# A gated convolution and token-mixing kernel: a new fixed order of the same operations, and some row work moved between VectorE and ScalarE

## The chip, the cores and the metric

The kernel runs on one core of a Trainium2 chip. A core has five engines that work side by side: TensorE (PE, matrix products), VectorE (DVE), ScalarE (ACT), GpSimd (POOL) and SyncE (SP), which here only issues transfers. Sixteen DMA engines move data between memory and the core's buffer; SP's transfers go through the queue called q1 in the profile, POOL's through q0. The metric is the device time of one execution in microseconds (us), the median of several runs.

## The reference

All inputs are bf16. S is 2048, D is 640, F is 1536. With x = q:

```python
# A: shift convolution of k, times v, then a long convolution per channel
k_shift = sum over t<4 of  k_pad[:, t:t+S] * shift_k[:, 3-t]
kv      = k_shift * v
y       = irfft(rfft(kv, 2S) * rfft(ssm_k, 2S))[:S]  +  kv * ssm_D
a       = q * y
# B: an MLP over the tokens
h = (x - mean) / sqrt(var + 1e-5)              # layernorm of each row
u = gelu(einsum("bsd,sf->bdf", h, w1) + b1)    # 2048 -> 1536
b = transpose(einsum("bdf,fs->bds", u, w2) + b2)
g = sigmoid(sum(x * gate_w))
out = g * a + (1 - g) * b
```

## The kernel before, in words

**How the work is tiled.** Rows of the 2048 tokens are spread over 128 partitions in four groups hk = 0 to 3 of four rows each, so that one tile of X holds 4 × 640 values per partition. The convolution is done by a 4096-point transform written as matrix products with two tables, FTB (forward) and GTB (back), split in four residues p = 0 to 3. The filter ssm_k comes in channel-major order and has to be transposed first (tiles wT, on PE, then copied out of PSUM by DVE or ACT).

**Stages, in the order in which they bind.**

1. Filter: load `ssm` in two halves of 1024 (each in two loads, of 2 and 3 channel blocks), transpose it (`transp`), transform it (`fwd`, `fwd_even`) into the tiles C. Beside it DVE takes the row statistics of X (`ln_tile`, L884 and L887), POOL raises the variance to −1/2 (`ln_scale`, sd and rstd), and DVE or ACT normalise the sixteen rows in place (`ln_apply`). POOL also makes the four gate factors KF.
2. The shifted k (`k_turn`, `kv`), its product with v, and the transform of that, with its sums over residues (`mixing`, `mixing_acc`; some of these sums are made by POOL, as transfers that add into their destination).
3. MLP, first product (m1): 12 tiles of F, each in 4 steps of 8 matmuls (L1083), with w1 in two ring buffers, ring0 and ring1, loaded in blocks c = 0, 1, 2 of four loads hk each (`w1_load`). ACT applies GELU into GT.
4. MLP, second product (m2): 16 tiles of the output, each in 6 steps of 4 matmuls (L1122), with w2 in the tile W2, loaded in two halves of six loads each (L1111). DVE meanwhile multiplies the two transforms (`product`, `cross`, `invmix`) and POOL adds pieces into C by accumulating transfers of 640 KB.
5. The transform back (`inverse`), times q and the gates, added to the MLP's result, stored in seven pieces and by four accumulating transfers.

W2 lies in the memory of ring0 and ring1 (W2's first 16 blocks are ring0, its last 16 are ring1). A load of W2 can therefore be issued only when the steps that read the old contents have ended: steps of m1 for the first contents, steps of m2 for the second half of w2.

**What sets the order.** `_build` makes a list of 712 operations. `_ORDER` is one list of their numbers, and `follow` (L299 on) puts the operations into that order; `emit` hands them out one by one, each to its engine's instruction stream, so an engine executes its operations in the order in which `_ORDER` names them. `_SLOTS` gives each of the 133 PSUM tiles one of four slots. `TAKES` says, for work that either DVE or ACT can do, which takes it: wT00 to wT14 (copies of transposed tiles out of PSUM, first digit the half), ln0 to ln15 (a layernorm row), kp0 to kp3 (a turn of k). `_Tracker` finds every overlap of buffers and puts the semaphore waits in; a wait stands in the stream of the engine that needs it, and whatever follows in that stream stays behind it. The helper lines that appear in the profile: L298 matmul, L267 accumulating transfer from POOL, L272 transfer from SP, L603 ACT, L559 and L573/L574 DVE or POOL, L613 a DVE copy out of PSUM.

Numbers of operations that are named further on:

| numbers | what |
|---|---|
| 4, 5, 6, 7 | SP loads of X for hk 0 to 3 |
| 8, 9 and 12, 13 | SP loads of ssm, first half and second half |
| 10, 11 | SP loads of FTB |
| 226 | POOL memset of KT, the border of the turned k |
| 237 | SP load of w1, block 1, hk 0 (ring1); read first by m1 step 419 |
| 244, 245, 297, 299 | POOL accumulating transfers into C, stage 2 |
| 394 to 397 | SP loads of w1, block 2, hk 0 to 3 (ring0); 394 is read first by m1 step 435 |
| 458 to 463 | SP loads of W2, first half |
| 520 to 525 | SP loads of W2, second half |
| 602, 607, 611 to 614, 619 | POOL accumulating transfers into C, stage 4 |
| 540 to 574 | m2 steps of the output tiles 9 to 15, among them 558, 569, 570, 571, 572 |

Of the kernel before, what the change touches and what calls it, by code (L numbers as in the profile page):

```python
# [13 lines left out]
ACT = mybir.ActivationFunctionType  # L14
# [5 lines left out]
class _Tracker:  # L20
# [235 lines left out]
    def dma(self, stream, out_ap, in_ap, semname, transpose=False, noncontig=False, accum=False, wait=()):  # L256
        reads = [in_ap] + ([out_ap] if accum else [])
        writes = [out_ap]
        if wait:
            self.pre(stream, list(wait), [])  # L260
        acc = self.pre(stream, reads, writes)
        engobj = self.eng[stream]
        sem = self.dma_sems[semname]
        if transpose:
            ins = engobj.dma_start_transpose(out_ap, in_ap)
        elif accum:
            ins = engobj.dma_start(out_ap, in_ap, accum_op=ALU.add, max_dma_last_dim=2560)  # L267
        elif noncontig:
            with self.nc.allow_non_contiguous_dma(reason="tiny"):
                ins = engobj.dma_start(out_ap, in_ap)  # L270
        else:
            ins = engobj.dma_start(out_ap, in_ap)  # L272
        ins.then_inc(sem, 16)
        self.dma_cnt[semname] += 16
        v = self.dma_cnt[semname]
        self.dma_hist[(semname, v)] = dict(self.known[stream])
        src = ("dma", semname, v)
        for reg, mode in acc:
            self.add_record(reg, mode, src)
        return v  # L280
# [128 lines left out]
def bass_gated_mix__ssm_conv_h3__mixer_token_mlp__prompt_kernel(  # L409
    nc, A_q, A_k, A_v, A_shift_k, A_ssm_k, A_ssm_D, B_x, B_w1, B_b1, B_w2, B_b2, gate_w, out  # L410
):
    with nc.Block() as blk:

        @blk.tensor
        def _(pe_engine):
            _build(nc, A_q, A_k, A_v, A_shift_k, A_ssm_k, A_ssm_D, B_x, B_w1, B_b1, B_w2, B_b2, gate_w, out)
# [24 lines left out]
def _build(nc, A_q, A_k, A_v, A_shift_k, A_ssm_k, A_ssm_D, B_x, B_w1, B_b1, B_w2, B_b2, gate_w, out):  # L441
    Bsz, S, D = A_q.shape
    F = B_w1.shape[1]
# [8 lines left out]
    with ExitStack() as es:  # L452
# [13 lines left out]
        def alloc(name, shape, dtype, at=None):  # L466
            size = mybir.dt.size(dtype)
            for s_ in shape[1:]:
                size *= s_
            if at is None:  # L470
                off = cur[0]
                cur[0] = (off + size + 63) // 64 * 64
            else:
                off = at
            assert off % 4 == 0 and off + size <= top, f"SBUF overflow {name}: {off}+{size} > {top}"
            h = nc.alloc_sbuf_tensor_at(name, list(shape), dtype, offset=off)
            T.reg_sbuf(h, off)
            return h
# [36 lines left out]
        ring = [alloc(f"ring{i}", [128, 16, 512], BF16) for i in range(2)]  # L515
# [90 lines left out]
        def either(name, default):  # L606

            return TAKES.get(name, default)

# [35 lines left out]
        def dma(o, i, nbytes, stream="SP", prio=None, sem=None, rate=365.0, tok=None, **kw):  # L645
            if sem is None:
                sem = f"d{ndma[0]}"
                ndma[0] += 1
            if sem not in T.dma_sems:
                T.add_dma_sem(sem, es.enter_context(nc.semaphore(f"s_{sem}")))  # L650
            rd = [i] + ([o] if kw.get("accum") else [])
            o_ = SC.add(stream, nbytes / rate / 1000.0, lambda s: T.dma({"QA": "ACT"}.get(stream, stream), o, i, sem, **kw), rd, [o], prio=prio, lat=-1.0, name="dma")
            if tok is not None:
                toks[tok] = o_
            return o_

        def dr(t, off, ap):
            return bass.AP(tensor=t.tensor, offset=t.offset + off, ap=ap)
# [22 lines left out]
            dma(X[:, hk, :, :], row8(A_q, hk), 128 * 5120, tok=f"x{hk}", rate=400.0)  # L681

        def w1_load(c, hk):
            dma(ring[c % 2][:, 4 * hk:4 * hk + 4, :], dr(B_w1, (1024 * (hk // 2) + 4 * (hk % 2)) * F + 512 * c, [[8 * F, 128], [F, 4], [1, 512]]), 128 * 4096, tok=f"w{c}{hk}")

        def k_load(hk):
            dma(kn[hk % 2][:, :, :], row8(A_k, hk), 128 * 5120, tok=f"k{hk}")
# [24 lines left out]
            dma(o, i, nbytes, stream=stream, **kw)  # L712

        SSM0 = ((0, 2), (2, 5))
        TAKES = {'wT00': 'DVE', 'wT01': 'DVE', 'wT02': 'ACT', 'wT03': 'ACT', 'wT04': 'ACT', 'ln0': 'ACT', 'ln1': 'DVE', 'ln2': 'DVE', 'ln3': 'DVE', 'ln4': 'DVE', 'ln5': 'ACT', 'ln6': 'DVE', 'ln7': 'DVE', 'ln8': 'ACT', 'ln9': 'ACT', 'ln10': 'ACT', 'ln11': 'DVE', 'ln12': 'ACT', 'ln13': 'ACT', 'ln14': 'ACT', 'ln15': 'DVE', 'kp0': 'DVE', 'kp1': 'DVE', 'wT10': 'ACT', 'wT11': 'DVE', 'wT12': 'ACT', 'wT13': 'ACT', 'wT14': 'ACT', 'kp2': 'DVE', 'kp3': 'ACT'}
        ORDER = "x0 s00 s02 x1 f0 f1 x2 x3 s10 s12 w00 w01 k0 k1 w02 w03 gw t0 t1 v0 v1 k2 k3 v2 v3 t2 t3 w10 w11 w12 w13 g w20 w21 w22 w23".split()
        LNSEQ = "s0 s1 a0 s2 a1 s3 a2 a3".split()
        LB = [0, 4, 8, 12, 16]
# [27 lines left out]
        for a, b in SSM1:  # L746
            ssm_load(1, a, b)
        w1_load(0, 0)
        w1_load(0, 1)

        zz = alloc("zz", [128, 512], BF16, at=base_of(GTB))
# [22 lines left out]
        for hk in range(2, 4):  # L774
            w1_load(0, hk)
# [294 lines left out]
        for ft in range(FT):  # L1070
# [16 lines left out]
            if ft in (1, 3, 5, 7):  # L1087
                hk = ft // 2
# [235 lines left out]


_ORDER = """
# [24 lines left out]
"""  # L1351
_SLOTS = "0323102030032211332223111230122113203310203131102102333312112310102123021121020211023120332002313302211002332213013220303301330301031"
# [1 line left out]
_INS = ['A_q', 'A_k', 'A_v', 'A_shift_k', 'A_ssm_k', 'A_ssm_D', 'B_x', 'B_w1', 'B_b1', 'B_w2', 'B_b2', 'gate_w']  # L1354
_OUTS = [((1, 2048, 640), 'bfloat16')]
# [23 lines left out]
```

## Time and profile before

| | before |
|---|---|
| median of 3 runs | 190.12 us (189.32 to 190.36) |
| profiled execution | 190.56 us, of which the span in the profile is 188.7 us |
| mean granted clock of TensorE | 0.982 |
| PE busy | 173.8 us, 92% of the span |
| DVE busy | 167.6 us, 89% |
| ACT busy | 113.0 us, 60% |
| POOL busy | 42.4 us, 22% |
| DMA | 45.60 MB, mean 242 GB/s |

The profile is of one execution. A row of a group names line, engine, operation, the tiles written and read, the count, the busy time, the mean length of one in ns, and the idle time before it with what ended it. Instructions overlap on an engine, so busy time divided by the count says how far apart they start. The view of slices gives 40 equal parts of the span (4.7 us each) in tenths. A time to landing runs from the issue of a transfer to its last byte.

### The profile page before, as it was taken

The page shows a single profiled execution, that of the slowest core. Times are in us where ns is not written, and L with a number is a line of the kernel's source. Part 1 is how long each engine was busy: PE and PEld are TensorE (multiplying, and loading weights), DVE is VectorE, ACT ScalarE, POOL GpSimd, SP SyncE. Part 2 cuts the span into 40 slices and gives each one's busy share as a digit, 9 for nine tenths or more (in the row PEclk, how much of TensorE's full clock was granted, in tenths as well). Part 3 has the DMA queues.
Part 4 walks back from the last instruction along what each step waited for, and adds up shares of the span by engine and source line. Part 5 has one row for each costly group of instructions (what it writes and reads, how often), then busy time and mean ns, then how long its engine had stood idle before and what let it go on. Part 6 is the DMA issues. An engine that isn't in the chain of part 4 may idle for free.

```text
span 188.7 us, 3258 instructions
## 1 busy us (share of the span) xinstructions
PE 173.8 (92%) x1347; PEld 133.0 (70%) x1348; DVE 167.6 (89%) x198; ACT 113.0 (60%) x176; POOL 42.4 (22%) x42
## 2 busy tenths in 40 slices
PE   7989888999999999997999999999956799999992
PEld 2657524786677667765777778999954499987782
DVE  2799989999899997999999999999999999009894
ACT  2589999999999999977163040041500105088780
POOL 1591067000005053003311102137300000005500
PEclk9999999999999999999999999999998599999999
DMA  4999999999799999999994629999999997004998
GB/s 172 373 407 401 389 221 213 390 416 200 132 295 309 221 203 196 196 260 345 196 190 129 122 47 367 268 237 205 187 236 255 318 416 310 0 0 72 204 278 285
DMA packets 32202, 45.60 MB, mean 242 GB/s; under 512 B 11705, under 2 KB 21050, under 8 KB 32188
## 3 DMA queue, kind: packets, MB, share of 16 engines
q1 hardware_dynamic: 26384, 32.94, 53.2%
q0 software_dynamic: 5744, 12.45, 37.2%
q8 instruction: 10, 0.16, 0.3%
q14 instruction: 4, 0.03, 0.0%
q10 hardware_dynamic: 60, 0.01, 0.0%
HBM read 27.70 MB, written 2.62 MB: 161 GB/s over the span
## 4 chain that ended last, share of the span: by engine, by line
PE 58%; ACT 18%; DMA 15%; DVE 5%; POOL 2%; issue 1%; DVEq 0%; SPq 0%
PE pp L298 58%; DMA W<-in_B_w_dram 9%; ACT C L603 6%; DMA ring<-in_B_w_dram 5%; ACT ksh L603 5%; ACT X L603 3%; DVE stats L884 2%; POOL rstd L559 2%; ACT wT L603 2%; ACT kp L698 1%; DVE C L559 1%; ACT GT L603 1%; DVE wT L613 1%; DVE kp L694 0%; DVE O L619 0%
## 5 line engine op out<-in xcount | busy, mean ns | idle before, releaser
L559 DVE TENSOR_TENSOR C<-C 128x2560 bf16<-128x2560 bf16 (+2 forms) x47 | 61.2, 1344 | 1.7 <-ACT C L603 1.4
L298 PE MATMUL pp<-GT,W 128*128 128x320 bf16 x384 | 57.5, 309 | 5.4 <-DMA W<-in_B_w_dram 5.4
L298 PEld LDWEIGHTS pp<-GT,W 128*128 128x128 bf16 x384 | 52.3, 146 | 9.5 <-DMA W<-in_B_w_dram 6.6
L298 PE MATMUL pp<-X,ring 128*128 128x320 bf16 x384 | 55.2, 299 | 1.3 <-DMA ring<-in_B_w_dram 1.0
L298 PEld LDWEIGHTS pp<-X,ring 128*128 128x128 bf16 x384 | 37.1, 98 | 16.4 <-DMA ring<-in_B_w_dram 1.3
L603 ACT ACTIVATE C<-pp 128x640 bf16<-128x640 f32 x64 | 40.5, 735 | 1.3 <-PE pp L298 1.1
L603 ACT ACTIVATE O<-pp,c,omg 128x640 bf16<-128x640 f32 x15 | 12.9, 881 | 42.3 <-PE pp L298 42.1
L267 POOL DMA_DIRECT2D C<-C x10 | 12.3, 1372 | 51.9 <-DVE C L559 45.2
L603 ACT ACTIVATE GT<-pp,cc 128x640 bf16<-128x640 f32 x12 | 9.6, 798 | 18.5 <-PE pp L298 18.5
L298 PE MATMUL pp<-wT,FTB 128*128 128x320 bf16 x112 | 17.9, 301 | 2.9 <-ACT C L603 1.4
L298 PEld LDWEIGHTS pp<-wT,FTB 128*128 128x128 bf16 x112 | 9.2, 97 | 11.1 <-ACT C L603 6.1
L559 DVE TENSOR_TENSOR tm<-C,C 128x2560 bf16<-128x2560 bf16 (+1 forms) x7 | 14.3, 2055 | 0.0
L603 ACT ACTIVATE cgb<-pp,gg 128x640 bf16<-128x640 f32 x16 | 12.2, 791 | 3.1 <-PE pp L298 1.8
L267 POOL DMA_DIRECT2D O<-q_hi x4 | 4.8, 1324 | 39.3 <-DVE q_hi L559 39.2
L884 DVE BATCH_NORM_STATS2 stats<-X 128x6 f32<-128x320 bf16 x32 | 13.2, 468 | 0.0
L559 DVE TENSOR_TENSOR q_hi<-cgb,q_hi 128x1280 bf16<-128x1280 bf16 x4 | 3.2, 822 | 10.1 <-ACT cgb L603 10.1
L267 POOL DMA_DIRECT2D C<-q_hi x6 | 5.9, 977 | 26.9 <-DVE q_hi L559 16.7
L559 DVE TENSOR_TENSOR SS<-C 128x2560 bf16<-128x2560 bf16 x8 | 11.7, 1483 | 0.0
L603 ACT ACTIVATE gq<-gq 128x640 bf16<-128x640 bf16 x16 | 11.7, 745 | 0.0
L559 DVE TENSOR_TENSOR C<-tm 128x2560 bf16<-128x2560 bf16 (+1 forms) x9 | 10.5, 1191 | 0.0
L603 ACT ACTIVATE ksh<-pp 128x1024 bf16<-128x1024 f32 (+1 forms) x12 | 10.4, 883 | 0.0
L298 PE MATMUL pp<-C,GTB 128*128 128x320 bf16 x64 | 9.8, 299 | 0.0
(72 smaller groups left out, 183.9 us busy)
## 6 DMA issues: line engine op xcount, KB each, us to landing
C<-C POOLq DMA_DIRECT2D x10, 640.0 KB, 8.9
ring<-in_B_w_dram SPq DMA_DIRECT2D x12, 512.0 KB, 9.3
W<-in_B_w_dram SPq DMA_DIRECT2D x12, 512.0 KB, 8.4
X<-in_A_q_dram SPq DMA_DIRECT2D x4, 640.0 KB, 9.6
kn<-in_A_k_dram SPq DMA_DIRECT2D x4, 640.0 KB, 12.8
out_dram<-O SPq DMA_DIRECT2D x7, 320.0 KB, 3.5
C<-SS POOLq DMA_DIRECT2D x3, 640.0 KB, 9.4
ssm<-in_A_ssm_k_dram SPq DMA_DIRECT2D x2, 768.0 KB, 9.1
```

The lines of the kernel that those rows point to most:

```text
L267: ins = engobj.dma_start(out_ap, in_ap, accum_op=ALU.add, max_dma_last_dim=2560)
L298: ins = self.nc.tensor.matmul(ps_ap, lhsT=lhsT, rhs=rhs, start=start, stop=stop, skip_group_check=True)
L559: o_ = SC.add(eng, d, lambda s: T.op(eng, lambda e: e.tensor_tensor(o, a, b, op), rd, [o]), rd, [o], prio=prio, name="tt")
L603: return T.op("ACT", lambda e: e.activation(o, src, func, **kw), rr + [src], ww)
L613: return T.op("DVE", lambda e: e.tensor_copy(o, src), [src], [o])
L698: o_ = SC.add("ACT", act_dur(2560), lambda s: T.op("ACT", lambda e: e.activation(ov, iv, ACT.Copy), [i[:, :, :]], [o[:, :, :]]), [i[:, :, ...
L884: ops.append(SC.add("DVE", 0.38, (lambda o, i: lambda s: T.op("DVE", lambda e: e.bn_stats(o, i), [i], [o]))(o, i), [i], [o]))
```

## The change

The order of the operations is a new one, and with it the PSUM slots. No operation is added or taken away, and no transfer changes its size. `TAKES` moves two transposed tiles from DVE to ACT (wT00, wT01), six layernorm rows from ACT to DVE (ln0, 5, 8, 9, 10, 14) and two from DVE to ACT (ln11, ln15). `w1_load` gets a rate, an operand that only states a duration for the drawing up of an order.

```diff
         def w1_load(c, hk):
-            dma(ring[c % 2][...], dr(B_w1, ...), 128 * 4096, tok=f"w{c}{hk}")
+            dma(ring[c % 2][...], dr(B_w1, ...), 128 * 4096, tok=f"w{c}{hk}", rate=325.0)
...
-        TAKES = {'wT00': 'DVE', 'wT01': 'DVE', 'wT02': 'ACT', 'wT03': 'ACT', 'wT04': 'ACT', 'ln0': 'ACT', 'ln1': 'DVE', 'ln2': 'DVE', 'ln3': 'DVE', 'ln4': 'DVE', 'ln5': 'ACT', 'ln6': 'DVE', 'ln7': 'DVE', 'ln8': 'ACT', 'ln9': 'ACT', 'ln10': 'ACT', 'ln11': 'DVE', 'ln12': 'ACT', 'ln13': 'ACT', 'ln14': 'ACT', 'ln15': 'DVE', 'kp0': 'DVE', ...}
+        TAKES = {'wT00': 'ACT', 'wT01': 'ACT', 'wT02': 'ACT', 'wT03': 'ACT', 'wT04': 'ACT', 'ln0': 'DVE', 'ln1': 'DVE', 'ln2': 'DVE', 'ln3': 'DVE', 'ln4': 'DVE', 'ln5': 'DVE', 'ln6': 'DVE', 'ln7': 'DVE', 'ln8': 'DVE', 'ln9': 'DVE', 'ln10': 'DVE', 'ln11': 'ACT', 'ln12': 'ACT', 'ln13': 'ACT', 'ln14': 'DVE', 'ln15': 'ACT', 'kp0': 'DVE', ...}
...
 _ORDER = """
-8 0 9 4 10 5 7 11 1 13 12 20 16 6 25 21 26 226 28 2 14 32 17 22 23 3 18 24 33 39 34 30 35 42 31 19 36 86 37 40 38 43
+4 0 8 1 20 16 9 21 2 32 17 23 5 3 10 6 7 11 13 12 94 26 36 90 45 14 18 88 25 19 97 15 34 91 27 92 96 39 37 35 22 87 93
...
-_SLOTS = "0323102030032211332223111230122113203310203131102102333312112310102123021121020211023120332002313302211002332213013220303301330301031"
+_SLOTS = "0331012303123112030221232321132013112002011211120100110301033011020310301031031300202300332231122033100233121200323113121020330030323"
```

What this does to the queues that issue transfers, in words:

- SP, start: X for hk 0 goes first, then ssm's first half, X for hk 1, the first table, X for hk 2 and 3, the second table, and then ssm's second half. Before it was ssm's first half, X 0, table, X 1 and 3, table, ssm's second half, X 2.
- SP, rings: 237 is issued last of its four loads (before first), 394 last of its four.
- SP, W2: 463 goes ahead of 461 and 462. The second half is issued as 520, 522, 523, 521, 524, 525 (before 520 to 525 in turn).
- POOL: the memset of KT goes behind the first rstd; the last five accumulating transfers of stage 4 ahead of the transform back go 613, 619, 614, 612, 611 (before 613, 619, 612, 614, 611).
- PE: the steps of m1, m2 and the transforms are interleaved anew. The number of matmuls between the step that frees a part of W2 and the step that first reads its new contents changes with that.

More of the change, by code (lines that the diff above doesn't have):

```diff
@@ L683, in w1_load @@
         def w1_load(c, hk):
-            dma(ring[c % 2][:, 4 * hk:4 * hk + 4, :], dr(B_w1, (1024 * (hk // 2) + 4 * (hk % 2)) * F + 512 * c, [[8 * F, 128], [F, 4], [1, 512]]), 128 * 4096, tok=f"w{c}{hk}")
+            dma(ring[c % 2][:, 4 * hk:4 * hk + 4, :], dr(B_w1, (1024 * (hk // 2) + 4 * (hk % 2)) * F + 512 * c, [[8 * F, 128], [F, 4], [1, 512]]), 128 * 4096, tok=f"w{c}{hk}", rate=325.0)
         def k_load(hk):
@@ L714, in _build @@
         SSM0 = ((0, 2), (2, 5))
-        TAKES = {'wT00': 'DVE', 'wT01': 'DVE', 'wT02': 'ACT', 'wT03': 'ACT', 'wT04': 'ACT', 'ln0': 'ACT', 'ln1': 'DVE', 'ln2': 'DVE', 'ln3': 'DVE', 'ln4': 'DVE', 'ln5': 'ACT', 'ln6': 'DVE', 'ln7': 'DVE', 'ln8': 'ACT', 'ln9': 'ACT', 'ln10': 'ACT', 'ln11': 'DVE', 'ln12': 'ACT', 'ln13': 'ACT', 'ln14': 'ACT', 'ln15': 'DVE', 'kp0': 'DVE', 'kp1': 'DVE', 'wT10': 'ACT', 'wT11': 'DVE', 'wT12': 'ACT', 'wT13': 'ACT', 'wT14': 'ACT', 'kp2': 'DVE', 'kp3': 'ACT'}
+        TAKES = {'wT00': 'ACT', 'wT01': 'ACT', 'wT02': 'ACT', 'wT03': 'ACT', 'wT04': 'ACT', 'ln0': 'DVE', 'ln1': 'DVE', 'ln2': 'DVE', 'ln3': 'DVE', 'ln4': 'DVE', 'ln5': 'DVE', 'ln6': 'DVE', 'ln7': 'DVE', 'ln8': 'DVE', 'ln9': 'DVE', 'ln10': 'DVE', 'ln11': 'ACT', 'ln12': 'ACT', 'ln13': 'ACT', 'ln14': 'DVE', 'ln15': 'ACT', 'kp0': 'DVE', 'kp1': 'DVE', 'wT10': 'ACT', 'wT11': 'DVE', 'wT12': 'ACT', 'wT13': 'ACT', 'wT14': 'ACT', 'kp2': 'DVE', 'kp3': 'ACT'}
         ORDER = "x0 s00 s02 x1 f0 f1 x2 x3 s10 s12 w00 w01 k0 k1 w02 w03 gw t0 t1 v0 v1 k2 k3 v2 v3 t2 t3 w10 w11 w12 w13 g w20 w21 w22 w23".split()
```

46 rows, old and new, of the table _ORDER are left out of this document.

## The prediction

> **What bounds the kernel now.** I read the shares first, then the chain of waits, then what TensorE (PE) waits for, and then the stretches in which it loses time. Shares and slices:
>
> ```profile
> PE 173.8 (92%) x1347; PEld 133.0 (70%) x1348; DVE 167.6 (89%) x198; ACT 113.0 (60%) x176; POOL 42.4 (22%) x42
> ...
> PE   7989888999999999997999999999956799999992
> ...
> PEclk9999999999999999999999999999998599999999
> DMA  4999999999799999999994629999999997004998
> ```
>
> PE and DVE are both near 90%. A slice is 4.7 us. PE has one deep hole, slices 30 to 32 (about 140 to 155 us), there the granted clock falls to half, and the DMA row reads 9. The chain that ended last, its end part (start, length, what):
>
> ```profile
> 76.43 10.29 DMA ring<-in_B_w_dram
> 86.77 25.75 PE pp L298 x188
> 112.53 4.70 DMA W<-in_B_w_dram
> 117.28 17.91 PE pp L298 x128
> 135.20 12.64 DMA W<-in_B_w_dram
> 147.89 37.54 PE pp L298 x260
> ```
>
> From 76 us on the chain is PE, broken only by three weight loads: one of w1 (ring) and two of w2 (W). PE's waits (total, times, longest) and DVE's largest:
>
> ```profile
> PE pp L298 <- DMA W<-in_B_w_dram: 5.4, 3, 3.8
> PE pp L298 <- DMA ring<-in_B_w_dram: 1.0, 1, 1.0
> ```
> ```profile
> DVE q_hi L559 <- ACT cgb L603: 10.1, 2, 9.7
> ```
>
> DVE, though 89% busy, stands still for 9.7 us near the end until PE has made its operand, so it does not set the end. What the stretches cost (start:end, length, busy and count by PE, PEld, DVE, ACT, POOL, then clock, DMA share, GB/s):
>
> ```profile
> 139.50:151.70 12.20, 7.13 (x33) 4.77 (x33) 12.16 (x11) 0.88 (x1) 0.00 (x0) 0.72 1.08 291
> 86.77:112.50 25.73, 25.73 (x190) 18.99 (x191) 25.73 (x26) 8.37 (x19) 5.86 (x6) 1.00 0.74 161
> 10.30:34.30 24.00, 21.08 (x163) 12.47 (x161) 22.98 (x63) 23.25 (x38) 11.53 (x11) 1.00 1.08 328
> 34.30:86.80 52.50, 50.57 (x466) 36.92 (x466) 50.07 (x44) 50.81 (x85) 7.48 (x6) 1.00 1.02 257
> ```
>
> Undisturbed, a matmul takes 25.73/190 = 0.135 us. The hole of 12.20 us held 33, worth 4.5 us: **7.7 us are lost there**, the largest single loss. PE around it, and the queues that led to it:
>
> ```profile
> 143.29 3.30 PE L298 MATMUL pp<-GT,W 128*128 128x320 bf16 x16 [3.77 <-DMA W<-in_B_w_dram]
> 147.89 4.37 PE L298 MATMUL pp<-GT,W 128*128 128x320 bf16 x18 [1.30 <-DMA W<-in_B_w_dram]
> ```
> ```profile
> 133.03 6.89 SPq L272 DMA_DIRECT2D W<-in_B_w_dram  x4
> ```
> ```profile
> 126.55 1.20 POOL L267 DMA_DIRECT2D C<-C  x1 [3.28 <-DMA C<-q_hi]
> 127.86 1.20 POOL L267 DMA_DIRECT2D C<-SS  x1
> 129.92 3.67 POOL L267 DMA_DIRECT2D C<-C  x3 [0.86 <-DMA C<-q_hi]
> ```
>
> Of the 7.7 us, 3.77 + 1.30 are idle and the other 2.6 are matmuls at half clock. SP issued the four loads of w2's second half (operations 522 to 525) between 133.03 and 139.92, just behind five accumulating transfers from POOL (613, 619, 612, 614, 611). The queues' shares of the DMA engines in 133 to 136.25, in 136.25 to 140.7 and in 145.3 to 150 (q0 is POOL's, q1 SP's):
>
> ```profile
> q0 software_dynamic: 254, 0.61, 107.7%
> ```
> ```profile
> q0 software_dynamic: 265, 0.64, 83.8%
> q1 hardware_dynamic: 177, 0.36, 23.7%
> ```
> ```profile
> q0 software_dynamic: 223, 0.53, 59.2%
> q1 hardware_dynamic: 415, 0.79, 47.1%
> ```
>
> For 3.2 us SP's loads get nothing, then a quarter, then a half: what was issued first goes first. Time from issue to landing of the w2 loads issued at 133.0, 135.2 and 137.4, of one issued at 101.1 (little traffic), and of the ring load issued at 76.0:
>
> ```profile
> DMA to landing us min/median/max: 10.2/10.2/10.2
> ...
> DMA to landing us min/median/max: 12.6/12.6/12.6
> ...
> DMA to landing us min/median/max: 13.3/13.3/13.3
> ...
> DMA to landing us min/median/max: 3.5/3.5/3.5
> ...
> DMA to landing us min/median/max: 9.2/9.2/9.2
> ```
>
> **The change, part by part.** All 712 operations and their bytes stay; their order on each engine, the PSUM slots and the engine of some row work change. The rate in the w1 load is an operand of the order's maker and emits nothing: 0.
>
> *W2, second half.* SP issues a load only after the PE steps that read the old contents. I counted matmuls on PE, in both tables, from the step that frees the rows to the first step that reads the load. Before: 48, 48, 64 and 60 (522, 523, 524, 525), that is 6.5, 6.5, 8.6 and 8.1 us at 0.135. After: 80, 104, 56 and 64, that is 10.8, 14.0, 7.6 and 8.6. The freeing of 522 also stands 36 matmuls (4.9 us) earlier, so with 523 and 521 behind it (521 is now the last of the three; its gap from its issue is 60 matmuls, 8.1 us) it is issued near 127, at the time of 619 and ahead of 612, 614 and 611. On POOL, 613 moves some 7 us earlier (by the work counted ahead of it), and 614 now goes ahead of 612. So these three no longer meet a full queue: no stall. 524 keeps its place on PE (1056 matmuls before it in both tables), is issued near 136.4, and is needed 7.6 us later by step 558. What it meets is what 522 met before: the last accumulates, outstanding, and no load ahead of it. So I take 522's 10.2 us: **a stall of 2.6 us**. Bounds: 3.5 us in a quiet queue gives no stall, 9.2 gives 1.6, 13.3 gives 5.7. 525 has its 8.6 plus the stall, 11.2, against 10.2: none; 521's stall, if there is one, lies inside 524's flight and does not add. The half clock came behind an idle time of 3.77, not behind the ring wait of 1.0; for 2.6 I charge nothing, at most 2.6. So 7.7 lost become 2.6: −5.1.
>
> [...]
>
> *Start.* Rows for it: SP's issue of X0, behind two loads of ssm; its time to landing; DVE's first statistics; the row work and the transposed tiles on both engines (count, then busy us).
>
> ```profile
> 1.73 0.49 SPq L272 DMA_DIRECT2D X<-in_A_q_dram  x1
> ```
> ```profile
> DMA to landing us min/median/max: 6.8/6.8/6.8
> ```
> ```profile
> 8.79 2.06 DVE L884 BATCH_NORM_STATS2 stats<-X 128x6 f32<-128x320 bf16 x5
> ```
> ```profile
> L603 ACT ACTIVATE X<-X,nm,rstd 128x640 bf16<-128x640 bf16 x8 | 7.0, 916 | 0.0
> L603 ACT ACTIVATE wT<-pp 128x1024 bf16<-128x1024 f32 x7 | 6.6, 1040 | 0.3 <-PE pp L298 0.3
> L613 DVE CAST wT<-pp 128x1024 bf16<-128x1024 f32 x3 | 3.7, 1225 | 1.3 <-PE pp L298 1.3
> L574 DVE TENSOR_SCALAR X<-X,mv,rstd 128x640 bf16<-128x640 bf16 x8 | 3.0, 433 | 0.0
> ```
>
> SP now issues X0 ahead of ssm. The two ssm loads ahead of it are 1.31 MB, at the 328 GB/s of the stretch from 10.3 to 34.3 some 4.0 us: X0 lands near 4.5 to 5 instead of 8.5, and DVE's statistics start near 4.9, 3.9 us earlier. ssm's first half comes later by X0's 0.66 MB, 2.0 us; its second half moves behind X for hk 2 too, also about 2 us. Two transposed tiles go from DVE (−2 × 1.23) to ACT (+2 × 0.94); layernorm rows go net four from ACT (−4 × 0.88) to DVE (+4 × 0.38). So ACT ends with 1.6 less and DVE with 1.0 less. In 10.3 to 34.3 ACT is full (23.25 of 24.0) and PE idles 2.9; the rows leave ACT only later, from 34.3 on, where it is full too (50.81 of 52.5). Later ssm (+2.0), less two tiles at 0.94 in place of 1.23 (0.6) and half of the 1.3 idle before DVE's tiles, is **+0.8** at 34.3. Bounds: −1.5 (DVE's lead and ACT's relief shorten what comes next) and +4 (2 us of later ssm and 1.9 of tiles both stay on ACT). POOL's moves (KT's memset, the gate factors KF, pieces of sd and rstd) are covered: POOL is busy 7.5 of 52.5.
>
> *Ring and W2, first half.* w1's third block has its load for hk0 last on SP; POOL's accumulates 297, 299, 245 and 244 are issued about 3 us earlier, so what held the load at 76.0 for 9.2 to 10.3 us is mostly gone, and its first reader stands where it stood: **−1.0** (bounds −1.0 and +2.3, if it takes 12.6). 463 is issued ahead of 461 and 462, which leaves each first-half load 7 us or more: **−0.4** (5.4 − 3.77 − 1.30), bounds −0.4 and +1.
>
> *End.* PE comes 5.7 us sooner to the inverse (5.1 + 1.4 − 0.8). DVE, which must have the products by then, gains 3.9 of start and 1.0 of work, 4.9. Cover short by 0.8: I take **+0.5**; bounds 0 and, if its lead were lost, 4. The stores and the order of the last evictions only swap places: 0.
>
> Sum: the profiled execution took 190.56 (span 188.7 and 1.86 around it), 0.44 above the median. 190.56 + 0.8 − 1.0 − 0.4 − 5.1 + 0.5 = 185.4, less 0.44: **184.9 us**.
>
> **The rivals.** *Equal shares (B).* If the loads take turns with the accumulates, 524 needs less than 7.6 us: 185.4 − 2.6 − 0.4 = 182.4. For it: 47% for q1 in 145.3 to 150; against it: 0 in 133 to 136.25. *The late start stays (D).* ACT is full to 86.8 and pays +4 instead of +0.8: 188.1. For it: 23.25 of 24.0; against it: row work leaves ACT. *No earlier than before (C), on the other side.* Three loads issued ahead put 1.57 MB before the accumulates, and 524 gets nothing until they are through, so it lands at 150.7 as before. Place: step 558. Its 136.4 to 150.7 is 14.3, a stall of 6.7, and half clock behind it, 2.6: 185.4 − 2.6 + 6.7 + 2.6 − 0.4 = 191.7. It decides from a landing of 13.7 us on (stall 6.1). For it: 13.3 for 524 before; against it: two loads were ahead of 524 then, and none now. *The order does next to nothing (E):* if the burst only shifts along, losses appear elsewhere in the same size: about 190.
>
> **How the numbers follow.** A difference of 0.5% is about what a measurement of this kernel can tell from none: faster is below 189.2, slower above 191.1. Chances: likeliest 0.50 (184.9; its own range 182.4, no stall, to 188.0, 5.7), B 0.12, D 0.14, E 0.06, C and like stalls 0.18. Faster: 0.50 + 0.12 + 0.09 of D = 0.71; same: E and 0.02 of D, 0.08; slower: C and the rest of D, 0.21. The range reaches from 181.3 (B, and the start's −1.5 in part) to 192.2 (C, and 0.5 of the ring's bound).
>
> **What would show it.** In the profile after: W2 loads 522, 523 and 521 issued near 127 and landed before step 570, 569 and 571 read them; one wait of PE for W of 2 to 3 us near 144; no clock at half; no wait for ring at 86; DVE's first statistics near 5; PE at 34 us less than 1.5 us behind. [...]

## The result, and the profile after

| | before | changed |
|---|---|---|
| median | 190.19 us (188.9 to 192.06, 20 runs) | 188.34 us (185.94 to 189.84, 20 runs) |
| ratio of the runs | | 0.9873, 95% interval 0.9842 to 0.9904 |
| profiled execution | 190.56 us, span 188.7 us | 189.44 us, span 187.6 us, mean clock 0.964 |

The kernel is faster by 1.3%; 184.9 us, 2.8%, was forecast. The ratio leaves out the runs that lie more than 1.5% above the fastest of their kernel, so it is not the quotient of the two medians. The direction holds, the size is less than half. In three later sets of runs, on three chips, the same kernel took 186.68, 186.92 and 187.64 us, with ratios to before of 0.9792, 0.9861 and 0.9866 (the experiments below), so about half of the gain that was forecast is there, in one set three quarters. The profiled execution stands 1.1 us above its own median; it is read here for where time is lost, and the terms are sized further down on a profile whose time, 186.93 us, stands near its median.

The same views as before, of the changed kernel. Shares and slices first:

```profile
PE 175.7 (94%) x1347; PEld 135.0 (72%) x1348; DVE 168.0 (90%) x200; ACT 111.3 (59%) x173; POOL 42.2 (23%) x42
...
PE   7699978999999999999999999999999499999993
...
PEclk9855999999999999999999999999999969999999
DMA  6999979999997999999999579898999999306997
```

The hole at slices 30 to 32 (counted from 1) has shrunk to one slice, the 32nd. A new loss stands at the other end: the clock is at half in slices 3 and 4 and low in slice 2, where the kernel before shows full clock. The chain that ended last, in order of time (start, length, what):

```profile
1.17 5.92 DMA ssm<-in_A_ssm_k_dram
7.09 0.05 issue
7.14 7.28 PE pp L298 x62
...
75.37 64.12 PE pp L298 x468
139.49 0.02 issue
139.51 10.50 DMA W<-in_B_w_dram
150.01 0.05 issue
150.06 29.32 PE pp L298 x200
```

Where three weight loads broke the chain of before from 76 us on, one is left: 524, issued at 139.51 and landed 10.50 us later. The chain now also begins with a load, the first of ssm, which lands at 7.09. (In the part left out stands one ring load, issued at 55.71 and landed 9.97 us later; PE waits 0.3 us for it.) What PE waits for (total, times, longest), then the stretches of both losses (start:end, length, busy and count of PE, PEld, DVE, ACT, POOL, then clock, DMA share, GB/s):

```profile
PE pp L298 <- DMA W<-in_B_w_dram: 2.7, 1, 2.7
PE pp L298 <- DMA ssm<-in_A_ssm_k_dram: 1.7, 1, 1.7
PE pp L298 <- ACT wT L603: 1.6, 3, 1.2
```
```profile
10.00:12.00 2.00, 2.00 (x16) 1.25 (x16) 1.30 (x4) 1.36 (x3) 0.00 (x0) 0.50 1.00 332
12.00:14.00 2.00, 2.00 (x17) 1.59 (x16) 2.00 (x7) 1.35 (x2) 0.00 (x0) 0.50 1.00 416
...
150.00:152.00 2.00, 1.94 (x11) 1.64 (x12) 2.00 (x3) 0.00 (x0) 0.00 (x0) 0.77 1.05 246
152.00:154.00 2.00, 2.00 (x10) 1.19 (x9) 2.00 (x2) 0.00 (x0) 0.00 (x0) 0.50 1.09 395
```

The stall that was forecast is there almost to the tenth: one wait for W, 2.7 us, at step 558. Behind it, though, stands a stretch at half clock, and behind the 1.7 us of waiting for ssm another one.

### The profile page after: what moved, and what is told of

The parts are those of the page before. It is cut to its first block, busy times and chain, and to the rows that moved or that the text cites. A ratio compares the mean times of both kernels' runs of the same rounds, so it can differ in the third digit from the quotient of the medians.

```text
span 187.6 us, 3260 instructions
## 1 busy us (share of the span) xinstructions
PE 175.7 (94%) x1347; PEld 135.0 (72%) x1348; DVE 168.0 (90%) x200; ACT 111.3 (59%) x173; POOL 42.2 (23%) x42
## 4 chain that ended last, share of the span: by engine, by line
PE 68%; DMA 14%; ACT 14%; SPq 2%; issue 1%; DVE 0%; DVEq 0%
PE pp L298 68%; ACT C L603 6%; DMA W<-in_B_w_dram 6%; DMA ring<-in_B_w_dram 5%; DMA ssm<-in_A_ssm_k_dram 3%; ACT ksh L603 3%; ACT wT L603 2%; ACT X L603 2%; SPq L272 2%; ACT kp L698 1%; ACT GT L603 0%; DVE O L619 0%; DVEq L412 0%; SPq L265 0%; ACT KT L603 0%
## 5 line engine op out<-in xcount | busy, mean ns | idle before, releaser
L298 PE MATMUL pp<-GT,W 128*128 128x320 bf16 x384 | 56.4, 306 | 2.7 <-DMA W<-in_B_w_dram 2.7
L298 PE MATMUL pp<-X,ring 128*128 128x320 bf16 x384 | 55.9, 299 | 0.3 <-DMA ring<-in_B_w_dram 0.3
L603 ACT ACTIVATE C<-pp 128x640 bf16<-128x640 f32 x64 | 41.3, 712 | 3.7 <-PE pp L298 3.4
L267 POOL DMA_DIRECT2D C<-C x10 | 12.8, 1567 | 58.2 <-DVE C L559 55.6
L298 PE MATMUL pp<-wT,FTB 128*128 128x320 bf16 x112 | 18.7, 316 | 1.9 <-ACT wT L603 1.2
L298 PEld LDWEIGHTS pp<-wT,FTB 128*128 128x128 bf16 x112 | 10.5, 103 | 9.6 <-ACT C L603 3.4
L559 DVE TENSOR_TENSOR SS<-C 128x2560 bf16<-128x2560 bf16 x8 | 12.5, 1580 | 2.6 <-ACT C L603 2.6
L559 DVE TENSOR_TENSOR tm<-C,C 128x2560 bf16<-128x2560 bf16 (+1 forms) x7 | 14.3, 2058 | 0.1
L603 ACT ACTIVATE wT<-pp 128x1024 bf16<-128x1024 f32 x9 | 9.0, 1035 | 4.1 <-PE pp L298 4.1
L559 POOL TENSOR_TENSOR KF<-cw,m 128x1120 bf16<-128x1120 bf16 x4 | 8.1, 2059 | 14.3 <-DVE mv L887 14.3
L559 DVE TENSOR_TENSOR C<-tm 128x2560 bf16<-128x2560 bf16 (+1 forms) x9 | 10.5, 1190 | 0.1
L267 POOL DMA_DIRECT2D C<-q_hi x6 | 6.4, 1204 | 18.0 <-DVE q_hi L559 14.7
## 6 DMA issues: line engine op xcount, KB each, us to landing
ssm<-in_A_ssm_k_dram SPq DMA_DIRECT2D x2, 768.0 KB, 10.6
```

Of the source, the lines that this page charges most:

```text
L298: ins = self.nc.tensor.matmul(ps_ap, lhsT=lhsT, rhs=rhs, start=start, stop=stop, skip_group_check=True)
L559: o_ = SC.add(eng, d, lambda s: T.op(eng, lambda e: e.tensor_tensor(o, a, b, op), rd, [o]), rd, [o], prio=prio, name="tt")
L603: return T.op("ACT", lambda e: e.activation(o, src, func, **kw), rr + [src], ww)
```

## The experiments

To see where an order gains or loses I read from each trace when PE begins the first step at or past a given number of matmuls. "Changed, again" is the changed kernel as it is, in a later execution. Times in us, and the difference to the profile of before:

| matmuls done | before | changed, profile of the result | changed, again (e5) | before, then after (e1) | early W2 (e7) | W2 between (e11) |
|---|---|---|---|---|---|---|
| 300 | 39.23 | +4.18 | +0.79 | +0.25 | +0.84 | +0.96 |
| 700 | 87.73 | +2.73 | +0.22 | +0.47 | +0.47 | +0.05 |
| 1056 | 137.05 | +2.13 | −0.38 | −0.12 | −0.24 | −0.23 |
| 1112 (step 558 in the new order) | 152.78 | −2.72 | −5.16 | −4.84 | −7.59 | −7.58 |
| 1152 | 158.21 | −1.12 | −3.62 | −3.23 | −7.59 | −7.58 |
| 1300 | 178.60 | −1.15 | −3.65 | −3.26 | −2.48 | −7.61 |

Theory S: the new start costs time (late ssm, a gap on PE, half clock), the new order around W2 gains it. Its rivals are in the expectations. The diffs below are shortened: of the order lists they show the operations that matter, and some between them are left out.

### One half of the order at a time (e1, e2)

An order may be cut at a step: the prefix of one, then what is left in the sequence of the other. The cut is m1 step 435.

```diff
 # e1: TAKES and the prefix from before, the rest from after; e2 the other way round
-_ORDER = after
+_ORDER = before[: before.index(435)] + [i for i in after if i not in prefix]
```

> The order of before up to m1 step 435 (the first step of w1's third block, at 87 us), then everything that is left in the order of after. Theory S (the new start costs, the new W2 part gains): in the two traces PE stands 2.7 us later at 700 matmuls in the new order, and gains 0.6 up to 1056 and 3.2 in the hole of W2; this kernel keeps the 3.8 and loses the 2.7, so about 186.4 us, 1.9 below the changed kernel. Rival W (the early delay is taken up again before the end, the W2 part alone sets what is gained): about 188.3, as the changed kernel.

> The other half: the order of after up to step 435, then what is left in the order of before, with its W2 loads. Theory S: 2.7 us slower than before, about 192.9. Rival W: no slower than before, 190.2. In both, PE waits for W near 140 to 150 as before (more than 4 us) and the clock falls to half there.

e1 took 186.43 us (before 190.16; ratio 0.9811, 0.9762 to 0.986), e2 190.94 (ratio 1.004, 0.9999 to 1.0082). So all of the gain lies behind step 435. e1's time is the one that theory S gave, but e5, which has the new start, comes within 0.3 us of it (186.68), so this does not speak for S. e2 did not lose the 2.7 us that theory S gave it: in its profile PE stands 0.81 us late at 300 matmuls and 0.17 early at 700. It begins exactly as the changed kernel does, so the 4 us of the first profile are not a property of the order alone.

### The start (e3, e6)

```diff
 # e3: X0 (4) behind ssm's first half (8, 9), as before
-4 0 8 1 20 16 9 21 2 32 17 23 5 ...
+0 8 1 20 16 9 4 21 2 32 17 23 5 ...
 # e6: the same, and the memset of cst (18) in front of the statistics (94, 90, ...)
+0 8 1 20 16 18 9 4 21 2 32 17 23 5 ...
```

> The changed kernel with one operation moved: the load of X for hk 0 is issued behind the two loads of ssm's first half, as before. Theory S, with the place that I name: X0 ahead of ssm lets the first ssm land at 7.1 instead of 4.4 us, PE stands idle 1.7 us before the first transpose and runs at half clock up to about 17; with ssm first that goes, PE is 2 to 4 us earlier at 150 matmuls, and the time is about 186.4. Rival (the lag comes from ACT, which has all five first transposed tiles, or from ssm's second half behind X2): ssm lands early, the lag stays within 1 us, time 188.

e3 took 190.30 us (ratio 1.0005, 0.9969 to 1.004), and its expectation fell for a reason that I had not seen. ACT's timeline of e3 (start, length, what, idle time before it and what ended it):

```profile
9.31 0.20 ACT L603 ACTIVATE cst<-cst 128x1 f32<-128x1 f32 x1 [5.75 <-DVE cst L628]
```

ACT's first instruction reads a constant that DVE sets. In the new order DVE does that behind the first statistics of X0; with X0 issued later, DVE waits for X0, the constant behind it, ACT behind the constant, and PE behind ACT's copies of the transposed tiles (3.1 us). Taking one item back from a drawn-up order had put a new wait in place of the old. e3 tells nothing on ssm; e6 puts that right.

> The changed kernel with X0 issued behind ssm's first half, and with DVE's memset of the constant that ACT's first instruction reads put ahead of the statistics of X0 (in the kernel with ssm first alone it stood behind them, and ACT stood still until 9.3 us). Theory S: no gap on PE, full clock, PE within 1 us of the kernel before at 300 matmuls, 186.4 us. Rival (ACT's five tiles or ssm's second half make the lag): PE 2 us or more late at 300 matmuls though the clock is full, 188.

e6 took 188.37 us (ratio 0.9907, 0.9873 to 0.9941), 1.7 above the changed kernel on the same chip (186.68). No half clock is recorded at the start and ssm is early, and yet PE is 3.2 us late at 300 matmuls. PE's and DVE's waits of e6 (the one for cst is the wait for the first matmul's zeros, 1.2 us in every profile; the others name it zz):

```profile
PE pp L298 <- ACT C L603: 1.8, 3, 1.4
PE pp L298 <- ACT wT L603: 1.6, 3, 1.2
PE pp L298 <- DVE cst L628: 1.2, 1, 1.2
PE pp L298 <- DVE rows L770: 1.1, 1, 1.1
```
```profile
DVE stats L884 <- DMA X<-in_A_q_dram: 6.9, 1, 6.9
```

The rest of the new order counts on X0 being early: DVE's statistics wait 6.9 us for it, and the small work behind them comes late to PE. So theory S fell in its first form: X0 at the head is not the mistake of the new start; with the order that follows, it is worth 1.7 us by these two medians.

### The speed of PE at the start (e4, e14, e9)

The kernel begins with matmuls on zeros, which nobody reads: NSPIN of them and two more. Every trace shows them at 634 ns each at first (the very first one at 607 in before, 606 in the first profile). The trace's records of the granted clock begin between 4.2 and 7.2 us (in e9 later), and those that come after that take 379 ns.

```diff
-        NSPIN = 9
+        NSPIN = 14      # e4, e14;  5 in e9
```

> The changed kernel with 14 in place of 9 matmuls on zeros at the start (0.43 us each, 2.1 us more), so that PE has no gap before the first ssm lands at 7.1. It tells the half clock from the late landing: if the half clock is what costs, the clock stays full from 7 to 17 us, PE is 2 us or more earlier at 150 matmuls, and the time is near 187; if the late landing costs, the clock is full but the time stays at 188.3 (within 0.5); if the low clock has another cause, it is half again between 8 and 17 us.

> The changed kernel with 14 matmuls on zeros, paired with the changed kernel. If the slow start is what spreads the changed kernel's runs, these spread less, and their median is 0.5 to 1.5 below where the changed kernel's runs are near 188, and equal within 0.4 where they are near 186.7.

> The changed kernel with 5 in place of 9 matmuls on zeros at the start: PE's gap ahead of the first ssm grows by 1.7 us (4 x 0.43) from the 1.2 to 1.7 us that it has. Nothing of the results changes. Theory S: a longer gap makes the half clock certain: clock at half from about 8 to 17 us, PE 3 us or more late at 300 matmuls, and the time 1.5 to 2.5 us above the changed kernel. Rival (the clock has nothing to do with the gap): full clock from 8 us on, time as the changed kernel, since the first ssm's landing does not move.

e4 took 186.96 us (ratio 0.9831, 0.9779 to 0.9883) and e14 187.09 (0.9866, 0.9822 to 0.991); the recorded clock is full up to the W2 stall in both profiles. e9 took 188.44 us (0.9913, 0.9873 to 0.9953), against 186.92 (0.9861, 0.98 to 0.9923) for the changed kernel on the same chip. In e9's profile PE is 2.9 us later at 300 matmuls than in e5; in the time the medians put the low speed at 1.5 us, the ratios at 1.0, and their intervals overlap. How fast PE runs is seen in the forty transposes of ssm, whose shape is the same in all kernels (here of before, of the first profile of the changed kernel, of its repetition e5, of e4 and of e9; busy, mean ns, idle before):

```profile
L298 PE MATMUL pp<-ident,ssm 128*128 128x128 bf16 x40 | 3.5, 231 | 0.0
```
```profile
L298 PE MATMUL pp<-ident,ssm 128*128 128x128 bf16 x40 | 5.0, 297 | 1.7 <-DMA ssm<-in_A_ssm_k_dram 1.7
```
```profile
L298 PE MATMUL pp<-ident,ssm 128*128 128x128 bf16 x40 | 3.5, 231 | 1.2 <-DMA ssm<-in_A_ssm_k_dram 1.2
```
```profile
L298 PE MATMUL pp<-ident,ssm 128*128 128x128 bf16 x40 | 3.6, 232 | 0.0
```
```profile
L298 PE MATMUL pp<-ident,ssm 128*128 128x128 bf16 x40 | 5.4, 314 | 2.4 <-DMA ssm<-in_A_ssm_k_dram 2.4
```

No gap or 1.2 us, 231 ns; 1.7 or 2.4 us, 297 or 314. The two slow starts differ. In the first profile the matmuls on zeros speed up at 4.3 us and the clock falls again at 7.7. In e9 the clock's records begin only at 15.48 us: with seven matmuls on zeros in place of eleven, and 2.4 us of gap behind them, PE had not come up to speed at all until then. The views print full clock where there is no record, so e9's row reads 9 there while the transposes take 314 ns. The duration of a known shape shows it.

### The changed kernel again (e5, e10, e13)

> The changed kernel as it is, on the same chip as the three that follow. Theory S: the clock falls to half in some executions only, where PE's gap ahead of the first ssm is long enough (1.7 us in the profile of the changed kernel, 0.5 and 0.3 in the kernel that begins alike and goes on in the order of before). So the profile shows either a gap over 1.5 us with half clock after it, and PE 4 us late at 300 matmuls, or a gap below 1 us with full clock and PE within 1 us. Rival: the clock is independent of the gap.

> The changed kernel once more, beside the two others. If chips and executions differ only in the early gap, its profile again has PE within 1 us of before at 300 matmuls where the gap is below 1.3 us, and its time is 186.7; where the gap is near 1.7, the clock falls and the time is 188 or more.

> The changed kernel once more, paired with the one with 14 matmuls on zeros on the same chip. If the 188.3 of the first set of runs came from PE running at half speed at the start in part of its executions, some of these runs stand near 188 and the rest near 186.5.

186.68 us (ratio 0.9792, 0.9741 to 0.9844), 186.92 (0.9861, 0.98 to 0.9923) and 187.64 (0.9866, 0.9827 to 0.9904). All three profiles have full speed at the start, with gaps of 0.8 to 1.2 us. So the slow start comes in some executions only. e14's median is 0.55 below e13's on the same chip and its runs lie closer together (186.99 to 187.76 against 185.94 to 189.44), but the two ratios to before are the same, 0.9866, so a gain by the longer warm-up is not shown. Not all of the spread is the start: e13's own profile, at full speed there, has a ring wait of 2.1 us where e5 has 1.2.

The timed runs leave no trace, but each has its mean granted clock on record. Half clock comes in steps of 3.41 us in the traces, and one step takes 0.009 off the mean. Of the 44 executions of the changed kernel (20, 6, 6 and 12), 8 read 0.998 or more, which leaves no room for such a step: their median is 186.29 us. 26 read 0.990 or 0.991, one step, as in e5's profile, where it stands behind the stall for W: 187.9. 10 read less, down to the 0.964 of the first profile: 188.5. The first set has 13 runs of 0.99 or more, and their median is still 187.98. So half clock at the start, as far as it is recorded, explains little of the 1.7 us by which the first set stands above e5; that 3 of e5's 6 runs read 0.998 or more explains some. A late speed-up as in e9 leaves no mark in the mean, and late landings leave none, so the rest stays open.

### What holds 524 (e8, e7, e11)

```diff
 # e8: three accumulating transfers are not issued
         for op in self.order:
+            if op.idx in (614, 612, 611):
+                continue
             op.emit(...)
 # e7: 466 and 467 directly behind 465; 524 and 525 as soon as their rows are free
 # (a number with a colon: matmuls ahead of that place)
-... 976: 465 514 485 486 507 487 515 508 ... 1052: 466 569 524 ... 1072: 467 468 525
+... 976: 465 466 467 514 485 486 507 487 515 508 524 ... 488 525 ...
 # e11: 466 and 467 behind 488, after 619 and 614 in the list
-614 488 622 518 ... 490 624 466 491 569 524 ... 467 468 525
+614 488 466 524 467 525 622 518 ... 490 624 491 569 ... 468
```

> The changed kernel without the accumulating transfers 614, 612 and 611 (three sums into C are left out, so the convolution's part of the output lacks them). It tells what holds 524: with those transfers gone, 524 lands 3.5 to 5.5 us after its issue instead of 10.5, step 558 does not wait, and the clock stays full from 140 us on. Rival: 524 is slow by itself or by SP's later loads, it still takes 8 us or more.

One execution: 182.32 us, its convolution part lacking three sums. 524 is issued at 137.0 in this kernel and in e5. Issue to landing in e8, then in e5:

```profile
DMA to landing us min/median/max: 3.5/3.5/3.5
```
```profile
DMA to landing us min/median/max: 10.6/10.6/10.6
```

Without the three transfers 524 lands in the time of a quiet queue, PE does not wait for W, and the clock is full throughout. What holds 524 is shown: the accumulates that were issued before it. It does not wait for all of them to end. In e5 POOL's queue had 110.5% and 108.1% of the DMA engines in 137 to 139 and 139 to 141, SP's none; in 145 to 147.57 it was 75.7% and 32.6%. So 524, issued at 137.00, landed at 147.57, behind 619, 614 and 612 (137.93, 141.68, 146.39) but ahead of 611, which was issued 3.3 us before it and landed at 151.30.

> The changed kernel with m2 steps 466 and 467 (the last readers of the rows that 524 and 525 write) moved up behind step 465, and 524 and 525 issued as soon as the rows are free: 96 and 100 matmuls (13 us) from issue to need in place of 56 and 64. If the stall at step 558 is the late issue, the wait for W goes, and with it the half clock behind it: 2.7 + 1.6 less, about 184 to 185 by the profile of the changed kernel. Rival (the loads then meet the accumulating transfers anyway, or 521 gets late): a wait for W of 2 us or more stays, time within 0.8 of the changed kernel.

e7 took 188.25 us (ratio 0.991, 0.988 to 0.9939), 1.6 more than e5, where 184 to 185 was expected. Up to 1152 matmuls PE does what was expected: no wait for W, full clock, 7.6 us ahead of before. By 1300 it has given 5.1 of them back. DVE's and PE's waits of e7:

```profile
DVE C L559 <- DMA C<-SS: 4.3, 1, 4.3
DVE SS L559 <- DMA C<-C: 2.0, 1, 2.0
```
```profile
PE pp L298 <- DVE SS L559: 1.8, 1, 1.8
PE pp L298 <- ACT cgb L603: 1.7, 1, 1.7
PE pp L298 <- DVE C L559: 1.0, 1, 1.0
```

524 was issued at 131.59, the last of four loads from 128.87 on and 0.2 us ahead of the accumulate 619. In 134 to 137 SP's queue has 82.5% of the engines and POOL's 1.3%. 619 then takes 11.3 us to land, against 6.4 in e5 (131.53 to 137.93); DVE waits 4.3 us for it, and PE at the end for DVE. The order of issue had only chosen who waits.

> The changed kernel with m2 steps 466 and 467 moved up only behind step 488, so that 524 and 525 are issued 2.7 and 4.9 us sooner, but behind the issue of the last accumulating transfers, not ahead of them as in the kernel with early W2 loads. Theory Q (what is issued first goes first, and the loads and the accumulates share one stretch of DMA time): 524 lands about when it is needed, PE's wait for W falls to 1 us or less and the clock stays full, while 619 and 614 land as in the changed kernel (6 to 10 us after issue), so DVE does not wait for them: 182 to 185 us, 2 to 4 below the changed kernel. Rival (any load that is issued sooner delays the accumulates by as much): DVE waits for C<-SS or C<-C 3 us or more, and the time is within 0.8 of the changed kernel.

e11 took 183.12 us (ratio 0.967, 0.9617 to 0.9723; before 190.26, the changed kernel 186.92 on the same chip). It differs from e7 mainly by 2.7 us in the time at which 524 is issued: 134.31, behind the accumulates, which were issued from 131.73 to 133.92 (522, 523 and 521 go 1.1 us sooner than in e7). 619 lands at 139.49, 7.8 us after its issue, 524 at 143.96. PE's stretch in e11, then its part behind the stall in e5, then DVE's waits of e11:

```profile
138.63 17.72 PE L298 MATMUL pp<-GT,W 128*128 128x320 bf16 x128 [0.43 <-ACT O L603]
```
```profile
147.61 12.70 PE L298 MATMUL pp<-GT,W 128*128 128x320 bf16 x80 [2.81 <-DMA W<-in_B_w_dram]
```
```profile
DVE C L559 <- DMA C<-SS: 0.8, 1, 0.8
DVE C L559 <- DMA C<-C: 0.3, 1, 0.3
DVE q_hi L559 <- ACT cgb L603: 0.3, 1, 0.3
```

Both sides get their data just in time, and the end keeps the 7.6 us: the time and the waits are those of theory Q. Its "what is issued first goes first" holds only in part: 524 lands ahead of 614, 612 and 611 (144.05, 149.16 and 155.52), which were all issued before it. DVE's wait for cgb, 9.7 us before the change, is down to 0.3, so DVE has no slack left there. e11 is the fastest kernel here.

### The ring wait (e12)

```diff
 # on top of e11: 237 is the first of its four ring loads
-238 231 29 240 239 237
+237 238 231 29 240 239
```

> The kernel with 524 and 525 moved up behind step 488, and with 237, the ring load that m1 step 419 reads first, issued first of its four and not last. In the changed kernel PE waits 1.0 to 1.2 us for it near 65. If that wait is on the path, it goes and the time falls by about 1, to 182; if PE only meets ACT's evictions or the next ring load there instead, the time stays at 183.1 within 0.5.

184.13 us (ratio 0.9685, 0.9628 to 0.9742; e11 has 0.967). The wait for ring goes, and another stands in the same place. PE's waits, e11 and then e12:

```profile
PE pp L298 <- DMA ring<-in_B_w_dram: 1.0, 1, 1.0
```
```profile
PE pp L298 <- ACT GT L603: 1.8, 2, 1.5
```

So no gain is seen: ACT comes 1.5 us late with a tile of GT. This profile of e12 also shows half clock from 9.7 to 13.1 us, behind a gap of only 0.46 us, and PE stands 1.4 us later at 300 matmuls than in e11. So it is not shown that ACT would be late by as much without that; e12 also ran on another chip than e11. A long gap is not needed for half clock at the start; what decides in a given execution is not settled.

## Why the prediction was right or wrong

By its terms, in us of the profile, against e5 (half speed at the start absent, time at the median) and against the first profile:

| term | forecast | e5 | first profile |
|---|---|---|---|
| start, to 300 matmuls | +0.8 | +0.8 | +4.2 |
| ring, 300 to 700 | −1.0 | −0.6 | −1.5 |
| W2, first half, 700 to 1056 | −0.4 | −0.6 | −0.6 |
| W2, second half, 1056 to 1152 | −5.1 | −3.2 | −3.2 |
| end | +0.5 | 0.0 | 0.0 |
| sum | −5.2 | −3.6 | −1.1 |

**Right.** The bound: PE, held by W2 loads behind accumulating transfers. 522, 523 and 521 came early and without a stall; 524 met the accumulates alone and took 10.5 us where 10.2 was taken, so the stall was 2.7 where 2.6 was forecast; e8 shows the cause: 10.6 with the three transfers, 3.5 without. Rival B's number (turns taken, so no stall) is out. Its mechanism is not: behind 4 us without any share, 524 did share the engines and landed before 611, as 522 had landed before (143.25) ahead of 614 and 611 (145.30 and 149.98), both issued sooner. "What was issued first goes first" was too strong a reading of before; taking 522's own time as the price was what made the term come out. The issue times around it were read less well: 613 moved 3.5 us earlier in e5, not 7, and 619 was issued 3.9 us behind 522 (131.53 and 127.64), not at its time. Rival C (14.3 us, slower than before) did not come. The end's +0.5 was 0.0.

**Wrong: "for 2.6 I charge nothing".** This is the step that failed in every profile of the changed kernel (the first, e5, e10, e13). The clock fell to half behind the stall, for 3.41 us, and PE lost 1.6 us between 1112 and 1152 matmuls (−2.72 to −1.12, and −5.16 to −3.62 in e5). With a stall of 2.8 for 2.6 it makes most of the 1.9 us by which W2's second half fell short (−3.2 for −5.1), the largest shortfall in e5's column. The timed runs bear the price out: a median of 186.29 where no step at half is recorded, 187.9 where one is. This price is about half of the 3.4 us between 184.9 and 188.34; how the other half divides between the start and loads that landed late stays open. I had the price and called it the upper bound; I put the limit between 1.0 and 3.77 us of idle time, the only two cases that before had, and took the value on the cheap side. That idle time alone sets a limit was an estimate of mine, and no run shows one: half clock stood behind stalls of 2.1 (e4) to 2.9 us (e1), in ten of the eleven profiles that have such a stall, and in the eleventh, e3, the clock stayed full behind 2.33 us.

**Wrong: the start had no price for PE's speed.** The term counted when ssm lands and what ACT has to do, and that was right (+0.8 in e5). It did not count that the matmuls on zeros end before ssm lands now, so that PE stands idle before its first transposes. Where the speed falls, the term is +4.2 at 300 matmuls and still +2.7 at 700. Rival D named the size (+4) and the place, but through ACT; the transposes' 297 and 314 ns show that it is PE's own speed. With the speed kept, the term as a whole is what was forecast; its parts were not measured one by one.

**Half wrong: the ring.** The wait for 394 near 86 went, as forecast. What became late next is 237, near 63: issued last of its four, it is waited for 1.2 us in e5 and 2.1 in e13. I had read the SP queue for one block of w1 and not for the other. In e12 that wait is gone and one for ACT, 1.5 us, stands there; whether ACT would be late without e12's slow start is not shown.

**The range and the chances.** 188.34 lies in the range, 181.3 to 192.2, and on the side given 0.71. That it lies there is in part luck: the upper end comes from rival C, which did not happen. The likeliest case's own range, 182.4 to 188.0, held the three medians of the repetitions but not the first. The cases did not hold a start at half speed beside a stall at half clock.

## What to carry to other kernels

Here what was issued first had the DMA engines nearly to itself at first (524 got nothing for 4 us in e5, and in the first profile, where POOL's queue had 109.1% of the engines from 139.51 to 143.51; the accumulates had 1.3% from 134 to 137 us in e7), and then both shared them. So the question for a fixed order is not how early a load can go but which of the two can wait; 2.7 us in the issue of 524 decided between 0.991 (e7) and 0.967 (e11) of the time before. An idle time of 2.1 to 2.9 us on TensorE was mostly paid twice, once as idle and once, 1.6 us, as the half clock behind it; a forecast has to give that a price. When one item of a drawn-up order is taken back, look on every engine at what was put behind it.

## What the runs showed of the hardware that I had not expected

- In all these traces the granted clock changes only in steps of 3.41 us from its first record on: half clock lasts 3.41, 6.83 (before) or 10.24 us (the first profile's start), and where the steps lie differs between executions. Behind a stall for W half clock came where PE had been busy for 0.16 to 0.39 of the step before (0.19 in e5, 0.38 in e4, whose stall is 2.1 us), and not in e3, where it was 0.46 (1.58 of 3.41 us, stall 2.33).
- At the start that share does not decide alone: gaps of 0.8 and 1.2 us went without half clock in three profiles, 1.7 us was followed by it from 7.7 to 17.9 us (0.49 of the step before), and 0.46 us by 3.41 us of it in e12 (0.81).
- PE starts at half speed (the same matmul on zeros took 634 ns and started every 0.43 us at first, 379 ns and every 0.21 us later), and the clock row does not show it, since it reads full where nothing is recorded: in e9 the records begin at 15.48 us, and the transposes before that took 314 ns against 231.
- Leaving out three accumulating transfers of 640 KB each took 4.4 us off the kernel (182.32 against 186.68 on the same chip, one execution), and 524's landing from 10.6 to 3.5 us.
